# Block products by sevens, summed by chained accumulation in PSUM banks, with an order table per step

## Chip, cores and metric

The kernel runs on one core of one Trainium2 chip. The metric is the device time of one execution in microseconds; the median of the runs is what counts.

## What is computed

The reference is attention over 4 batches of 12 heads, 448 positions and 64 dimensions, followed by two dense layers on the 1792 x 768 result:

```python
x = attention(rmsnorm(q, g_q), rmsnorm(k, g_k), v)   # to [1792, 768]
h = x @ moe_w_in                                     # [768, 2048]
x = (h * sigmoid(h)) @ moe_w_out                     # [2048, 768]
h = x @ moe2_w_in
return (relu(h) ** 2) @ moe2_w_out
```

Inputs are float32. Each matmul operand is split into an upper part (a rounded copy) and a lower part (the rest), and every product is made of three matmuls: upper by upper, lower by upper, upper by lower.

## The kernel before

After attention (up to 223.8 us of the profile) comes layer one in eight segments ("seg": two halves of the 1792 rows, four quarters of the 2048 hidden columns), and then layer two ("end": two halves of the rows, each with eight groups of 2 x 128 hidden columns). A half is two batches of 448 rows, so a moving operand has 448 columns.

**Units.** The product of two blocks of hidden columns with two blocks of the 768 inputs and two batches of rows is an 8-product block product that is made with seven (`seven`, L1197). Its operands are sums of the weights' quarters (`four`, L1153) and of the rows' blocks (`combine`, L1343). Each of the seven products (`prod`, L1199 to L1218) is nine matmuls of 128 x 448, L1209. Product p1 (B11) is copied out of its bank to a tile (`p1_copy`, L604), the other products' banks are added to that tile or to further ones by VectorE (`u_sum`, L1224), and `finish` applies the activation and splits the result. B21 is accumulated in p1's bank behind B11. There are 14 such units in layer one and 16 in layer two.

**Down products.** In layer one (`down`, L1307) a product with the output weights is 12 matmuls of 448 columns, added to a running sum by VectorE (L1320). In layer two a group adds to `total`, 7 chunks of 128 rows by 768 columns. Done plainly (`plain`, L1543) it takes 14 blocks of six matmuls of 384 columns, L1550, each followed by an addition to `total` (`acc`, L1569). In the second half, groups 0 to 6 (`SEVEN2`) take seven products for eight here too (class `products7`, L1573): six of the seven chunks form three pairs, and for each pair products 1 to 7 of three matmuls each, L1674, are made from sums of the hidden blocks (`h_sum`, L1606) and of the output weights (`weights`, L1626). Each product's bank is added to `total` or to four further running sums; the remaining chunk is done plainly. `join` (L1712) adds these running sums up after the last of the seven groups.

**Weights.** The split output weights of layer two (tile w, 768 KB) are stored to a DRAM buffer su in the first half and loaded from it in the second (L1067, L1054); the second half's groups by sevens also load the unsplit words once more.

**Banks.** PSUM's eight banks are split in three rings after attention: "s" (four) for down products, "t" (three) for the seven products, "pv" (one) for p1.

**Halved matmuls.** `columns` (L1106) splits the second matmul of a product in two of 224 columns: in `seven` in products B11 and T4, in `up` always, in `down` in every third output block.

**Order.** Nothing is written in its final order by hand. Every step (a group of instructions with reads and writes) is recorded, and `Plan.forward` (L251) places steps on the engines' queues, taking at each turn the step that can start earliest and, between equals, the one due first. The due times come from a backward pass and tables of offsets by kind of step (`DUE`, `SHIFT`). The queue of an engine is in order: a step that waits holds up those behind it. Attention's steps have fixed nominal times.

Of the kernel before, what the change touches and what calls it, by code (L numbers as in the profile page):

```python
# [9 lines left out]
F32 = mybir.dt.float32  # L10
# [100 lines left out]
class Step:  # L111
# [13 lines left out]
ROUNDS = 8  # L125
AHEAD = 25.0
DUE = {
    "end0": {"acc": 4.25, "down2": -1, "h_hi": 21.25, "h_lo": 3.75, "keep_parts2": -1.25, "load_y": -0.75, "p1_copy": 3.75, "prod": 0.25, "square": 1, "u_sum": -0.5, "w_hi2": -6, "w_lo2": -0.75, "w_sum": -0.75, "y_hi": 5.25, "y_lo": 4.25, "y_sum": -3.5},
    "end1": {"acc": 2, "down2": -11.25, "h_hi": 16, "h_lo": 2.5, "h_sum": -39.5, "join": 18, "keep_parts2": -11.75, "load_parts2": -2.25, "load_word2": 1.75, "load_y": 0.5, "p1_copy": 0.5, "prod": 2, "square": 21.25, "store": -1.25, "u_sum": -1, "w_hi2": 4.25, "w_sum": -4.5, "y_lo": -3, "y_sum": 2.5},
    "now": {"ident": 5.75, "swap_pools": -0.5},  # L130
    "seg0": {"add": -0.5, "down": 3, "g_hi": 0.5, "g_lo": 0.75, "keep": 10.25, "load_raw": -6, "load_y": 0.5, "low": 1, "magnitude": -2, "merge": -6, "out1": -1, "p1_copy": 4, "part": 0.5, "prod": 4.75, "silu": 0.5, "store_y": -1, "u_sum": 2.75, "up": 2.5, "w_hi": 4.5, "w_lo": 6.25, "w_sum": -2, "y_hi": 0.75, "y_lo": 1, "y_sum": 2},
    "seg1": {"add": -4.25, "down": -4.5, "g_hi": 2.25, "g_lo": 5, "keep2": 45.25, "load_raw2": 6, "load_word": -5.5, "load_y": -0.75, "low2": -1.5, "magnitude2": -3, "merge2": -4.5, "p1_copy": -6.25, "part": -3.75, "prod": -3.25, "silu": -5.75, "store_y": 7, "u_sum": 2.25, "w_hi": 1.75, "w_lo": 1, "w_sum": -3, "y_hi": 10, "y_lo": 0.75, "y_sum": 2.5},
}

SHIFT = {
    "seg0": {"down": -3.25, "g_hi": 49, "g_lo": 4.75, "keep": -8.25, "load_raw": -17.5, "load_y": 21.5, "low": -35.5, "merge": 2.5, "part": 20.75, "silu": -0.5, "up": 2.5, "w_lo": 1.25, "y_lo": 3.75, "y_sum": 5.25},
    "seg1": {"add": -11.75, "down": -6, "g_hi": 148, "g_lo": -10.5, "keep": -27.75, "load_raw": -10.5, "low": -7.5, "magnitude": -17.25, "p1_copy": -4.25, "prod": 78.25, "u_sum": 123, "w_hi": 285.25, "w_lo": 29.75, "w_sum": -30.75},
    "seg2": {"add": 1.5, "down": -99.75, "g_hi": 30, "g_lo": 8, "keep": 22.25, "load_raw": -18.75, "low": -73.75, "magnitude": -0.25, "merge": -0.25, "p1_copy": -42, "prod": 14.5, "silu": 17, "u_sum": 27.75, "w_hi": -10, "w_lo": -55, "w_sum": -52.75},
    "seg3": {"down": -205.5, "g_hi": -6.5, "g_lo": 90.25, "keep": 33.25, "load_raw": 1.75, "low": -2.25, "magnitude": -1.25, "merge": -26.5, "out1": -8.5, "p1_copy": -9.5, "prod": 86, "silu": -1.75, "store_y": 4.5, "u_sum": -384.5, "w_hi": -37.75, "w_lo": 31.75, "w_sum": 1.75},
    "seg4": {"down": 9.25, "g_hi": -0.75, "g_lo": -3.25, "keep2": -23.75, "load_raw2": -7.25, "load_word": -15, "load_y": 8, "low2": 2.25, "magnitude2": 1, "merge2": 10.5, "p1_copy": 28.25, "part": 13.5, "prod": 2, "silu": -2, "w_hi": -2.75, "w_lo": 10.75, "w_sum": -13.5, "y_hi": 15.5, "y_lo": -406.5, "y_sum": 155},  # L140
    "seg5": {"add": -41, "down": 69.5, "g_hi": 72.25, "g_lo": 2.5, "keep2": -16, "load_raw2": -136.75, "load_word": -5.5, "low2": 77.25, "magnitude2": -29.5, "merge2": 163.25, "p1_copy": 3.5, "prod": 29, "silu": 10, "u_sum": -10.5, "w_hi": 17.75, "w_lo": 10.25, "w_sum": -101.75},
    "seg6": {"add": 11.75, "down": -291.75, "g_hi": 23.5, "keep2": -10.5, "load_raw2": 0.75, "load_word": -0.75, "low2": 7.75, "magnitude2": 66.75, "merge2": -52.75, "p1_copy": -37.25, "prod": 132, "silu": 193.5, "u_sum": -30.25, "w_hi": 23.25, "w_lo": -29.75, "w_sum": 9.5},
    "seg7": {"down": -5.75, "g_lo": 43.5, "keep2": -43, "load_raw2": 11.5, "load_word": -1.5, "low2": 17.25, "magnitude2": -5, "merge2": 49, "p1_copy": -1.75, "prod": -31, "silu": -27.25, "store_y": -18.25, "u_sum": -169, "w_hi": 57.5, "w_lo": -67.75, "w_sum": -132.25},
    "end-2": {"load_y": -17.25, "y_hi": 328.25, "y_lo": -2, "y_sum": 24.75},
    "end0": {"acc": 0.5, "down2": 3, "h_lo": -10.25, "load_word2": 4.25, "load_y": 4.5, "p1_copy": 4.25, "prod": 57, "relu": 13, "square": 6.75, "u_sum": 0.75, "w_hi2": -3.25, "w_lo2": 3.5, "w_sum": 14.75, "y_hi": 19.75, "y_lo": 21.5, "y_sum": -3.75},
    "end1": {"down2": -28, "h_hi": -1.25, "h_lo": -43.75, "keep_parts2": -19, "load_word2": 34.5, "p1_copy": 10.25, "prod": 0.25, "relu": 34, "square": -41.5, "u_sum": -6.25, "w_hi2": 79, "w_lo2": 89.5, "w_sum": -16},
    "end2": {"acc": -23.75, "down2": 6.5, "h_hi": 55.25, "h_lo": 1.25, "keep_parts2": 8.75, "load_word2": 3, "p1_copy": 21, "prod": 63, "relu": -16.25, "square": 0.5, "u_sum": -2.25, "w_hi2": 17.75, "w_lo2": -57, "w_sum": -15.25},
    "end3": {"acc": 4.25, "down2": 5, "h_hi": -80.5, "h_lo": 0.5, "keep_parts2": 59, "load_word2": 5.25, "p1_copy": 4.25, "prod": 3.5, "relu": -88.75, "square": 16.75, "u_sum": -28.5, "w_hi2": -9.5, "w_lo2": 22.75, "w_sum": -0.25},
    "end4": {"acc": 5.5, "down2": -14.25, "h_hi": 24.25, "h_lo": -11.25, "keep_parts2": 18.25, "load_word2": 10.25, "p1_copy": -69.25, "prod": -4.5, "relu": 5.5, "square": -7.5, "u_sum": 6, "w_hi2": -41.5, "w_lo2": -39.25, "w_sum": 39.25},
# [1641 lines left out]
```

## Time and profile before

| | us |
|---|---|
| median of 3 runs | 1115.44 (1114.39 to 1116.83) |
| profiled execution | 1114.12 |
| its span | 1112.3 |
| attention, up to the first matmul of layer one | 223.8 |
| last matmul starts | 1108.4 |

The span is the time from the first to the last instruction of the profiled execution; the execution's own time is 1.8 us more. The sum of a prediction is made against the profiled execution, which lies 1.3 us below the median. An engine's busy time counts its recorded instructions; matmuls are pipelined, so consecutive ones overlap in the record and their starts give the pitch.

### The profile page before, as it was taken

The numbers are of one execution on the slowest core, as the hardware profiler recorded it, in microseconds if no ns is written. First come the engines' busy times: TensorE is split into PE (matmuls) and PEld (weight loads), VectorE is DVE, ScalarE is ACT, GpSimd is POOL, SyncE is SP. The second block draws the span as 40 slices with busy tenths as digits, with TensorE's granted clock in tenths as the row PEclk, the third lists the DMA queues.
The fourth block names the chain that finished last, engine by engine and source line by source line (L and its number), as shares of the span: only waits on it lengthen the run. The fifth ranks groups of instructions, "written<-read, shape, count | busy, mean of one in ns | idle before, by whom it ended". The sixth has DMA issues, their size and how long they took to land.

```text
span 1112.3 us, 20308 instructions
## 1 busy us (share of the span) xinstructions
PE 1094.0 (98%) x7463; PEld 991.0 (89%) x7463; DVE 910.7 (82%) x1629; ACT 615.9 (55%) x1308; POOL 287.0 (26%) x361
## 2 busy tenths in 40 slices
PE   8999999999999999999999999999999999999998
PEld 6877777699999998999999989999999899999997
DVE  7999999857969689877767896787888877888886
ACT  7999999955645466455445544544333444333221
POOL 5789997300000012000102210022020311222220
PEclk9999999999999999999999999999999999999999
DMA  7344543377655568678776598877878874555453
GB/s 190 102 127 143 150 128 106 116 247 262 195 167 190 177 198 262 199 240 281 252 241 223 177 304 306 302 281 254 317 249 301 276 277 185 185 185 187 169 188 125
DMA packets 122435, 235.29 MB, mean 212 GB/s; under 512 B 12216, under 2 KB 86112, under 8 KB 122336
## 3 DMA queue, kind: packets, MB, share of 16 engines
q1 hardware_dynamic: 122096, 233.80, 63.2%
q8 instruction: 59, 0.97, 0.4%
q14 instruction: 40, 0.33, 0.1%
q10 hardware_dynamic: 240, 0.20, 0.1%
HBM read 157.58 MB, written 76.37 MB: 210 GB/s over the span
## 4 chain that ended last, share of the span: by engine, by line
PE 87%; DVE 7%; issue 2%; ACT 1%; DMA 1%; SPq 0%; POOL 0%; DVEq 0%; ACTq 0%
PE bank L1209 29%; PE bank L1307 20%; PE bank L1550 13%; PE bank L901 7%; PE bank L1674 6%; PE bank L791 4%; PE bank L834 3%; PE bank L1120 3%; PE bank L725 2%; DVE g L1224 1%; PE bank L798 1%; DVE w L625 1%; DVE gg L625 1%; DVE W L1030 1%; DMA w<-sz 0%
## 5 line engine op out<-in xcount | busy, mean ns | idle before, releaser
L1307 PE MATMUL bank<-gg,w 128*128 128x448 f32 (+1 forms) x1168 | 238.3, 363 | 2.4 <-DVE gg L625 1.4
L1307 PEld LDWEIGHTS bank<-gg,w 128*128 128x128 f32 x1168 | 216.3, 188 | 21.5 <-DVE gg L625 2.1
L1224 DVE TENSOR_TENSOR g<-bank,g 128x448 f32<-128x448 f32 x180 | 109.2, 620 | 53.0 <-PE bank L1209 47.9
L1550 PE MATMUL bank<-w,gh 128*128 128x384 f32 (+1 forms) x564 | 142.8, 334 | 0.9 <-DVE gh L618 0.9
L1569 DVE TENSOR_TENSOR gg<-bank,gg 128x384 f32<-128x384 f32 (+1 forms) x197 | 103.7, 551 | 25.0 <-PE bank L1550 24.5
L1209 PE MATMUL bank<-yb,w 128*128 128x448 f32 (+1 forms) x548 | 118.1, 363 | 0.5 <-ACT g L1277 0.5
L616 ACT CAST w<-W 128x768 fp32r<-128x768 f32 (+1 forms) x86 | 64.4, 752 | 96.2 <-PE bank L1550 28.1
L1209 PE MATMUL bank<-xb,w 128*128 128x448 f32 x528 | 115.2, 364 | 0.0
L625 DVE TENSOR_TENSOR w<-W,w 128x768 fp32r<-128x768 f32 (+1 forms) x121 | 105.8, 880 | 6.0 <-ACT w L616 4.9
L1209 PEld LDWEIGHTS bank<-yb,w 128*128 128x128 f32 x548 | 101.3, 188 | 8.6 <-ACT g L1277 0.8
L1209 PEld LDWEIGHTS bank<-xb,w 128*128 128x128 f32 x528 | 98.1, 188 | 7.9
L1550 PEld LDWEIGHTS bank<-w,gh 128*128 128x128 f32 x564 | 101.9, 188 | 2.1 <-DVE gh L618 1.3
L813 DVE TENSOR_REDUCE mx<-bank 128x1 f32<-128x448 f32 x168 | 96.4, 606 | 0.0
L1475 ACT ACTIVATE g<-g 128x448 f32<-128x448 f32 x48 | 27.7, 578 | 123.9 <-DVE g L1224 123.7
L1550 PE MATMUL bank<-w,gl 128*128 128x384 f32 (+1 forms) x282 | 94.2, 334 | 0.0
L821 ACT ACTIVATE E<-bank,mx 128x448 f32<-128x448 f32 x144 | 93.3, 705 | 0.7 <-DVE mx L813 0.2
L625 POOL TENSOR_TENSOR gl<-g,gh 128x448 fp32r<-128x448 f32 (+1 forms) x16 | 14.6, 914 | 188.3 <-ACT gh L616 110.1
L1023 ACT ACTIVATE raw<-raw 128x768 int32<-128x768 uint16 (+1 forms) x72 | 59.5, 826 | 3.0 <-DMA raw<-in_moe_w_in_dram 2.1
L1209 PE MATMUL bank<-xc,w 128*128 128x448 f32 x270 | 59.9, 366 | 0.0
L791 PE MATMUL bank<-T 64*128 64x448 f32 x432 | 54.8, 382 | 2.3 <-ACT T L734 2.1
L625 POOL TENSOR_TENSOR gg<-g,gg 128x448 fp32r<-128x448 f32 x6 | 7.9, 1315 | 183.7 <-ACT gg L616 176.3
L1209 PEld LDWEIGHTS bank<-xc,w 128*128 128x128 f32 x270 | 50.7, 188 | 4.3
(184 smaller groups left out, 2250.7 us busy)
## 6 DMA issues: line engine op xcount, KB each, us to landing
raw<-in_moe_w_in_dram SPq DMA_DIRECT2D x32, 768.0 KB, 5.1
raw<-in_moe_w_out_dram SPq DMA_DIRECT2D x24, 512.0 KB, 4.0
raw<-in_moe_w_out_dram SPq DMA_DIRECT2D x16, 768.0 KB, 6.0
su<-w SPq DMA_DIRECT2D x16, 768.0 KB, 6.3
w<-su SPq DMA_DIRECT2D x16, 768.0 KB
xf<-y SPq DMA_DIRECT2D x48, 224.0 KB, 5.0
xf<-x SPq DMA_DIRECT2D x39, 224.0 KB, 4.9
ki<-W SPq DMA_DIRECT2D x16, 384.0 KB, 6.1
```

Source lines behind the costliest of these rows:

```text
L616: nc.scalar.copy(o(), a())
L625: kind, when, any_t(n, rate), lambda e: engine(e).tensor_tensor(o(), a(), h(), ALU.subtract),
L791: nc.tensor.matmul(pts[j].ap[:, :S], T.ap[r, 0, a, c * CQ:(c + 1) * CQ], T.ap[r, 1, b_], start=(k_ == 0), stop=(k_ == 2),)
L813: lambda e, pt=pt, mx=mx: nc.vector.tensor_reduce(mx.ap, pt.ap[:, :S], AX.X, ALU.max, negate=True),
L821: lambda e, j=j, n=n, pt=pt, mx=mx, E=E: nc.scalar.activation(E.ap[:, j], pt.ap[:, :S], AF.Exp, bias=mx.ap, accum_out=sums.ap[:, n:n + 1]),
L901: nc.tensor.matmul(pv.ap[j * D:(j + 1) * D, q0:q0 + nq], vr.ap[:, j * NCH + m, :], pt.ap[:, j * NCH + m], start=(m == 0), stop=(m == NCH - ...
L1209: nc.tensor.matmul(pt.ap[:, c1:c2], w_()[:, c0 + c, :], view(b, a, c)()[:, c1:c2], start=(start and c == 0 and k == 0), stop=(c == HC - 1 ...
L1224: lambda e: nc.vector.tensor_tensor(o.ap, pt.ap[:, :S], a.ap, ALU.add),
L1307: nc.tensor.matmul(pt.ap[:, c1:c2], w_()[:, f, :], gg.ap[:, k, a, f, c1:c2], start=(f == 0 and n == 0), stop=(f == HQ - 1 and n == 2), ski ...
L1550: nc.tensor.matmul(pt.ap[:, :en], g.ap[:, fi, c0:c0 + P], w_()[:, 0, e0:e0 + en], start=(n == 0), stop=(n == 5),)
L1569: "acc", at, dve_t(n), lambda e: nc.vector.tensor_tensor(o(), pt.ap[:, :n], o(), ALU.add),
L1674: nc.tensor.matmul(pt.ap[:, :NH], a[i][0](m), b[j][0](), start=(start and k == 0), stop=(k == 2), skip_group_check=True,)
```

## The change

1. The groups 1, 3 and 5 of layer two's first half take seven products as well; in the second half the same seven groups do as before.
2. In `seven` the products B11, T2, T3 and T4 are accumulated one behind the other in p1's bank, and the running sum is copied out between them (`take`); T1 and B22 share the bank p5, B21 has p2. Three copies and three additions take the place of one copy and six additions.
3. In `products7.down` the products of a pair share two banks: 1, 6, 7, 4 follow each other in one, 5 and 3 in another (2 has a bank of its own before). Behind each product the bank is added to one block of `total`. The further running sums and `join` go.
4. The split output weights are no longer stored in DRAM; in both halves they are split from the words, which are loaded once per group and serve the sums too.
5. `columns` counts matmuls: it halves the second matmul of a product when more than 150 whole ones have passed, or when matmuls of 384 columns came between.
6. Rings of banks: "s" four and "t" four in layer one; "bu" three, "bv" two and "bx" three in layer two.
7. The due time of every step behind attention is read from a table `LATEST`, one number per step, kind by kind; the backward pass and the offsets go.

```diff
-SEVEN2 = (1,)
+SEVEN2 = {0: (1, 3, 5), 1: range(7)}
+LIST = [(1, 0), (1, 1), (1, 2), (2, 0), (2, 1), (6, 0), (6, 1), (2, 2), (6, 2), (5, 0), (7, 0), (5, 1), (7, 1), (3, 0), (7, 2), (3, 1), (5, 2), (4, 0), (4, 1), (3, 2), (4, 2)]
+KEEP = 150
-BANKS = {"any": (0, 8), "s": (0, 4), "t": (4, 3), "pv": (7, 1)}
+BANKS = {"any": (0, 8), "s": (0, 4), "t": (4, 4), "bu": (0, 3), "bv": (3, 2), "bx": (5, 3)}
...
+LATEST = {
+    "acc": [937, 1072, -3118, 1243, -2011, 894, -2156, 2509,
...
     def schedule(self):
...
+            due.append(-0.25 * LATEST[s.kind][turn[s.kind]])
...
+    since = [KEEP]
+    def columns(second):
+        since[0] += 1
+        if second and since[0] > KEEP:
+            since[0] = 0
+            return [(0, S // 2), (S // 2, S)]
+        return [(0, S)]
...
+        def take():
+            o = sb([P, S], F32, "g")
+            copy_step("p1_copy", at, ("act", "dve"), lambda: o.ap, lambda: p1.ap[:, :S], S, [p1], [o])
+            return o
+        p1, p2, p5 = (psum("t" if at[0] == "seg" else "bx") for _ in range(3))
         product(p1, w0, 0, "B11")
...
+        u1 = take()
+        product(p2, w0, HC, "B21")
+        product(p1, z, HC, "T2", False)
+        u2 = take()
+        product(p5, z, 0, "T1")
+        product(p1, v_, 0, "T3", False)
+        u3 = take()
+        plus(u3, p5)
+        product(p1, a22, 0, "T4", False)
+        c21 = sb([P, S], F32, "g")
+        product(p5, v_, HC, "B22", False)
+        finish(1, 1, u3)
+        finish(1, 0, c21, p1)
+        plus(u1, p2)
+        finish(0, 0, u1)
+        plus(u2, p5)
         finish(0, 1, u2)
...
-                wo = [parts(lambda f=f: second_out(f, at), DM, DM, at, f"u{f}") for f in (f0, f1)]
+                W2 = [second_out(f, at, "V", "yp") for f in (f0, f1)]
+                wo = [parts(lambda W=W: W, DM, DM, at) for W in W2]
...
+            C = {1: (0, 0), 2: (0, 0), 6: (0, 1), 5: (1, 1), 7: (1, 1), 3: (0, 1), 4: (1, 0)}
+            rows = [psum("bu") for m in range(self.npair)]
+            other = {}
+            for n, m in LIST:
+                if n in (2, 5):
+                    other[m] = psum("bv")
+                p = other[m] if n in (2, 5, 3) else rows[m]
+                product(n, m, p, n in (1, 2, 5), t)
+                t += DOWN2 / 4
+                to(*C[n], m, p, n)
```

(`plain` and the products of `products7` set the count of `columns` to 150, so the next product's second matmul is halved.)

The written order shows how the steps move. First the products of a unit on TensorE, in layer two's first half. Before (bank and tile names with their numbers; yb, xb, xc and part hold sums of the rows, w and v those of the weights):

```order
L1209 MATMUL bank5_10711<-yb_8968,w_10624 128x448 x9
L1209 MATMUL bank6_10724<-xb_8964,w_10641 128x448 x9
L1209 MATMUL bank4_10737<-xb_8983,v_10610 128x448
L1209 MATMUL bank4_10737<-xb_8983,v_10610 128x224 x2
L1209 MATMUL bank4_10737<-xb_8983,v_10610 128x448 x7
L1209 MATMUL bank7_10627<-xb_9111,w_10509 128x448 x9
L1209 MATMUL bank5_10774<-xc_9208,w_10624 128x448 x9
L1209 MATMUL bank6_10794<-part_9327,w_10641 128x448 x9
```

In the changed kernel, one of the four places with T3 and T4 next to each other:

```order
L1157 MATMUL bank5_9286<-yb_8917,w_9110 128x448 x9
L1157 MATMUL bank6_9310<-xb_9097,w_9110 128x448
L1157 MATMUL bank6_9310<-xb_9097,w_9110 128x224 x2
L1157 MATMUL bank6_9310<-xb_9097,w_9110 128x448 x7
L1157 MATMUL bank5_9286<-yb_8965,w_9220 128x448 x9
L1157 MATMUL bank7_9346<-xc_9218,w_9220 128x448 x9
L1157 MATMUL bank5_9286<-xb_8884,w_9282 128x448 x9
L1157 MATMUL bank5_9286<-xb_9002,v_9106 128x448 x9
L1157 MATMUL bank7_9346<-part_9308,w_9282 128x448 x9
```

Before, every product but B21 goes to a bank of its own. Now the products to bank5_9286 (B11, T2, T3, T4) stand with one product between them, and the last two with none; on ScalarE the sum behind T3 is copied between them:

```order
L546 COPY g_9323<-bank5_9286 128x448
...
L546 COPY g_9372<-bank5_9286 128x448
L1417 ACTIVATE g_9372<-g_9372 128x448
L1423 ACTIVATE g_9372<-g_9372 128x448
L1417 ACTIVATE g_9403<-bank5_9286 128x448
```

What moved: T4 waits for that copy, which waits for T3's last matmul.

Second, the down products by sevens on TensorE. Before, in the second half of layer two:

```order
L1674 MATMUL bank3_12217<-xb_11339,part_11678 128x384 x3
L1674 MATMUL bank0_12223<-xb_11339,part_11678 128x384 x3
L1674 MATMUL bank1_12229<-xb_11339,part_11678 128x384 x3
L1674 MATMUL bank2_12234<-xb_11339,part_11678 128x384 x3
L1674 MATMUL bank3_12241<-xb_11339,part_11678 128x384 x3
L1674 MATMUL bank0_12246<-xb_11339,part_11678 128x384 x3
```

In the changed kernel, in group 1 of the first half, where a group done plainly stood before (raw holds sums of the weights, part and R those of the hidden blocks):

```order
L1621 MATMUL bank3_9781<-raw_9717,part_9699 128x384 x3
L1621 MATMUL bank4_9787<-raw_9717,part_9699 128x384 x3
L1621 MATMUL bank1_9662<-raw_9777,part_9699 128x384 x3
L1621 MATMUL bank3_9781<-w_9600,part_9699 128x384 x2
L1621 MATMUL bank3_9781<-w_9600,R_9755 128x384
L1621 MATMUL bank4_9787<-w_9600,part_9699 128x384 x2
L1621 MATMUL bank4_9787<-w_9600,R_9755 128x384
L1621 MATMUL bank1_9662<-raw_9717,part_9699 128x384 x3
```

What moved: before, the four banks go round and a bank is written again behind three other products. Now bank3_9781, bank4_9787 and bank1_9662 are each written again behind two, with VectorE's addition of the bank to `total` between.

## Rows read from the trace of the kernel before

**Rows 1.** The page: the span, and the engines' busy time (share of the span).

```profile
span 1112.3 us, 20308 instructions
...
PE 1094.0 (98%) x7463; PEld 991.0 (89%) x7463; DVE 910.7 (82%) x1629; ACT 615.9 (55%) x1308; POOL 287.0 (26%) x361
```

**Rows 2.** Stretches: length, busy us of PE, PEld, DVE, ACT, POOL; PEclk; DMA share; GB/s.

```profile
223.80:685.70 461.90, 459.09 (x2308) 424.04 (x2307) 364.54 (x610) 239.66 (x391) 45.34 (x31) 1.00 0.70 230
685.70:882.00 196.30, 194.34 (x1055) 187.15 (x1054) 158.93 (x276) 85.43 (x146) 30.48 (x18) 1.00 0.78 277
882.00:1108.50 226.50, 223.90 (x1200) 211.93 (x1198) 181.52 (x346) 77.28 (x148) 45.34 (x42) 1.00 0.56 196
```

**Rows 3.** TensorE's timeline in layer one: start, us, what; three products between these.

```profile
363.21 1.99 PE L1209 MATMUL bank<-xb,w 128*128 128x448 f32 x9
...
368.68 7.58 PE L1307 MATMUL bank<-gg,w 128*128 128x448 f32 x36
```

**Rows 4.** TensorE's timeline in layer two; x10 is a product with a halved matmul.

```profile
900.35 2.02 PE L1209 MATMUL bank<-xb,w 128*128 128x448 f32 x9
902.21 2.00 PE L1209 MATMUL bank<-xb,v 128*128 128x448 f32 x10
904.05 1.99 PE L1209 MATMUL bank<-part,w 128*128 128x448 f32 x9
905.88 0.34 PE L1674 MATMUL bank<-xb,gh 128*128 128x384 f32 x1
...
906.94 0.33 PE L1674 MATMUL bank<-xb,gh 128*128 128x384 f32 x1
```

**Rows 5.** TensorE's timeline around a product between plain down products.

```profile
749.32 0.51 PE L1550 MATMUL bank<-w,gh 128*128 128x384 f32 x2
...
749.84 2.02 PE L1209 MATMUL bank<-yb,w 128*128 128x448 f32 x9
751.69 0.51 PE L1550 MATMUL bank<-w,gh 128*128 128x384 f32 x2
...
752.22 0.51 PE L1550 MATMUL bank<-w,gh 128*128 128x384 f32 x2
```

**Rows 6.** Groups by line (count, busy us, mean ns, idle before), whole span, then 685.7 to 882.

```profile
L1224 DVE TENSOR_TENSOR g<-bank,g 128x448 f32<-128x448 f32 x180 | 109.2, 620 | 53.0 <-PE bank L1209 47.9
...
L1569 DVE TENSOR_TENSOR gg<-bank,gg 128x384 f32<-128x384 f32 x84 | 44.6, 552 | 13.5 <-PE bank L1550 13.3
L625 DVE TENSOR_TENSOR w<-W,w 128x768 fp32r<-128x768 f32 x32 | 30.6, 970 | 0.1
```

**Rows 7.** Timelines of TensorE, VectorE and ScalarE, one after the other, 938 to 943 us.

```profile
938.48 2.00 PE L1209 MATMUL bank<-raw,w 128*128 128x448 f32 x10
940.32 0.51 PE L1674 MATMUL bank<-w,gh 128*128 128x384 f32 x2
...
941.73 0.34 PE L1674 MATMUL bank<-w,gl 128*128 128x384 f32 x1
942.42 0.59 PE L1674 MATMUL bank<-w,gh 128*128 128x384 f32 x2 [0.35 <-issue]
...
940.30 1.54 DVE L625 TENSOR_TENSOR xb<-V,xb 128x768 fp32r<-128x768 f32 x1
941.77 1.47 DVE L1569 TENSOR_TENSOR xf<-bank,xf 128x384 f32<-128x384 f32 x3
...
940.57 0.53 ACT L604 COPY g<-bank 128x448 f32<-128x448 f32 x1 [0.64 <-PE bank L1209]
```

**Rows 8.** TensorE's waits: us in total, times, longest.

```profile
PE bank L1674 <- issue: 0.3, 1, 0.3
```

**Rows 9.** DMA issues by tile, then TensorE's timeline at the turn of layer two's halves.

```profile
su<-w SPq DMA_DIRECT2D x16, 768.0 KB, 6.3
w<-su SPq DMA_DIRECT2D x16, 768.0 KB
...
878.25 2.09 PE L1209 MATMUL bank<-raw,w 128*128 128x448 f32 x10 [1.96 <-DMA w<-sw]
```

More of the change, by code (lines that the diff above doesn't have):

```diff
@@ L236, in link @@
                         pre[s.n][t.n] = True
-        late = {b.turn % BANKS["any"][1]: b for b in self.rings["any"]}
-        for tag, (first, n) in BANKS.items():
-            for b in self.rings[tag][:n] if tag != "any" else ():
-                for t in late[first + b.turn].steps:
-                    pre[b.first.n][t.n] = True
+        late = {}
+        for tags in STAGES:
+            last = dict(late)
+            for tag in tags:
+                first, n = BANKS[tag]
+                for b in self.rings[tag]:
+                    k = first + b.turn % n
+                    if b.turn < n and k in last:
+                        for t in last[k].steps:
+                            pre[b.first.n][t.n] = True
+                    late[k] = b
         for s in self.steps:
@@ L420, in stage @@
-        def stage(s):
-            when = s.when[0]
-            return when + str(int(s.when[1] >= {"seg": NQ, "end": self.turn}[when])) if when in ("seg", "end") else when
-        moved = [DUE.get(stage(s), {}).get(s.kind, 0.0) for s in steps]
-        due = [d + x for d, x in zip(due, moved)]
-        best = None
-        got = [None]
-        for _ in range(ROUNDS):
-            end = got[0]
-            got = self.forward(due, end)
-            if best is None or got[0] < best[0]:
-                best, args = got, (due, end)
-            late = self.backward(got[1], got[2])
-            due = [x - y for x, y in zip(moved, late)]
-            self.log = getattr(self, "log", []) + [round(got[0], 1)]
@@ L436, in part @@
-        def part(s):
-            when = s.when[0]
-            if s.nom is not None or when not in ("seg", "end"):
-                return None
-            return when + str(int(s.when[1] if when == "seg" else s.when[1] * 8 / self.turn))
-        due, end = args
-        return self.forward([d + SHIFT.get(part(s), {}).get(s.kind, 0.0) for s, d in zip(steps, due)], end)
+        turn = dict.fromkeys(LATEST, 0)
+        due = []
+        for s in self.steps:
+            if s.nom is not None:
+                due.append(0.0)
+                continue
+            due.append(-0.25 * LATEST[s.kind][turn[s.kind]])
+            turn[s.kind] += 1
@@ L445, in issue @@
+        assert all(len(LATEST[k]) == n for k, n in turn.items())
+        return self.forward(due, END)
     def issue(self):
@@ L1103, in ahead @@
         units.append(at)
-    def columns(halved):
-        return [(0, S // 2), (S // 2, S)] if halved else [(0, S)]
+    since = [KEEP]
[5 more added lines that the diff above has]
+        return [(0, S)]
     def up(x, w, gh, gl, keys, at, cuts):
@@ L1207, in products @@
                     for k, (w_, a) in enumerate(((wh, 0), (wl, 0), (wh, 1))):
-                        for c1, c2 in columns(c == 0 and k == 1 and n in ("B11", "T4")):
+                        for c1, c2 in columns(c == 0 and k == 1):
                             nc.tensor.matmul(
@@ L1305, in products @@
                             for n, (w_, a) in enumerate(((wh, 0), (wl, 0), (wh, 1))):
-                                for c1, c2 in columns(f == 0 and n == 1 and k == 0 and e_ % 3 == 0):
+                                for c1, c2 in columns(f == 0 and n == 1):
                                     nc.tensor.matmul(
@@ L1545, in products @@
         def products(e):
+            since[0] = KEEP
             n = 0
@@ L1573, with __init__ @@
     class products7:
-        def __init__(self, total, left, npair):
+        def __init__(self, total, left, npair, half):
             self.total, self.left, self.npair = total, left, npair
             self.part = sb([P, 2 * NC6 * S // 2], FR, "part", None, "yp")
-            self.block = sb([P, 2 * HC * S], FR, "xb")
-            self.word = [sb([P, UW], FR, "W") for _ in range(2)]
-            self.more = {(n, m): sb([P, S], F32, "xf") for m in range(npair) for n in ("U2", "P7")}
             L = left
@@ L1585, in at @@
                 return lambda: b.ap[:, c0:c0 + n]
+            last = sb([P, S], FR, "R", 2)
             self.S = {
```

255 lines of the change are left out of this document (75 added, 180 removed), and 6 rows, old and new, of the table LATEST.

## Prediction

> **What bounds the kernel now.** I read the first part of the page, then the stretches, then TensorE's timeline, and only then the other engines. The page shows TensorE busy for 98% of the span [rows 1]. The stretches show the same outside attention: TensorE stands idle for 2.8 us of 461.9 in layer one, 2.0 of 196.3 in layer two's first half and 2.6 of 226.5 in the second, with the clock granted in full, while VectorE has 19 to 21% of its time free and ScalarE 48 to 66% [rows 2]. So a matmul left out is time won, work on the other engines costs nothing unless a matmul waits for it, and the little that can be lost is lost in waits. The idle time, 7.4 us, understates these: a matmul is recorded with 0.36 us but the next starts 0.20 later, so about 0.16 of each pause is covered; with some twenty pauses, and 0.1 more before the pitch is back, I put all waits behind attention at about 12 us (an estimate).
>
> The timeline also shows two pitches for the same matmul of 448 columns. In layer one 27 of them take 5.47 us, 0.2026 each [rows 3]. In layer two nine take 1.86, 0.2067 each, until a product with a halved matmul: that one takes 1.84, and the next 1.83 [rows 4]. A stretch that enters from 384-column matmuls is slow, one behind a halved pair is fast.
>
> **The change, part by part.**
>
> *Matmuls left out.* A group of layer two done plainly takes 14 blocks of 6 matmuls, 84 of 384 columns; by sevens 21 products of 3 and 2 blocks of 6, 75. Three groups change: 27 matmuls fewer. Three take 0.52 us, 0.173 each [rows 5]: **−4.7 us**, in places where TensorE is the bound.
>
> *Halved matmuls.* Before, halving follows the name of a product; now the first product behind 384-column matmuls is halved at its second matmul, and otherwise one in some 150. In the written order 458 whole matmuls of 448 columns stand on the slow side before and 51 after: 407 × 0.0041 = −1.7. A halved pair costs 1.84 − 9 × 0.2026 = 0.017 [rows 4]; there are 66 for 84: −0.3. Leaving a fast stretch costs 0.02 (1.06 us for six of 384 columns [rows 4] for the usual 1.04), a slow one 0.01 [rows 5]; before, 27 and 13, now 52 and 0: +0.4. Together **−1.6 us**.
>
> The Trainium skill gives one pitch only ("TensorE: Matmul & The Clock Gate", Back-to-back issue gap): columns over 2.4 GHz plus 2.5 ns, so 189 ns for 448 columns and 162.5 for 384. By that, estimated from that page, the first term would be 4.4 us and this one nothing, together −4.4. The rows differ from it in both, and they decide.
>
> *Sums in banks.* Of the seven products of a unit four now go one after the other into one bank, and ScalarE or VectorE copies the sum out between them: three copies and three additions (30 units) for one copy and six additions. On VectorE layer two loses 46 additions of 0.62 [rows 6], 28.5 us, and ten joins of some 0.6. It gains 33 accumulations of 0.55, 18.2 us [rows 6], and 24 splits of 768 columns of 0.97 [rows 6], 23.3, since output weights are split anew in both halves instead of stored and loaded. Sum: about +7 on the 340 us that VectorE works in layer two [rows 2], so near 83% there, with more of it in the second half. ScalarE gains 26 copies of 0.53 [rows 7], 14 us, and has half its time free. All this I cost at nothing, because matmuls cover it; without that cover it is the third rival below.
>
> *The order of a bank's writes.* Four times in the new order (two in layer one, two in layer two's first half) product T4 stands right behind T3 in the same bank with the copy of that bank between. No such place exists before, so I price it from the nearest rows: the last matmul of a product starts 0.2 before the next row, at 940.12, its copy at 940.57, 0.45 later, and takes 0.53; a matmul that waited started 0.10 behind the read's end (941.77 + 0.55, 942.42) [rows 7]. So 1.08 for a usual 0.20, and 0.08 more for the next pair (0.59 for 0.51 [rows 7]): 0.96 each, **+3.8 us** if all else stays. Lower bound: nothing, where TensorE would have stood idle there for operands anyway, as it does in both layers now.
>
> *Transfers.* Sixteen stores and sixteen loads of 768 KB of split output weights go [rows 9], two loads of 384 KB come: 24 MB of 235 less, and the SP queue is shorter by 30 issues. The one visible wait of TensorE for a load is 1.96 us for w<-sw at the turn of the halves [rows 9]. It may go (−2.1 with its slow restart) or come back elsewhere, since that turn's order is new; bounds −2.1 and +2.1, taken at 0.
>
> *The other waits.* The order of every step behind attention is new, so each of today's waits is redrawn. Price from below: if only the four places and the last group's wait stay, about 8 less. From above: all 12 stay and the four come on top, with some late reads. I take the middle: the new order also holds about 12 us of waits, the four among them. The four are there because nothing else could be started, which is what the present waits are too.
>
> Sum: −4.7 − 1.6 = −6.3. The profiled execution took 1114.12 us and becomes 1107.8; it lies 1.3 below the median shown, so the median becomes **1109.1 us**. Attention, up to 223.8 us, has the same instructions in the same order on every engine.
>
> **Rivals.**
>
> *More goes than the matmuls.* The waits fall to about 4 us, because fewer transfers and fewer additions leave operands ready: 1109.1 − 8 = 1101. For it: half of VectorE's additions to units are gone. Against: it is no less busy in all.
>
> *The saving is eaten.* The four places come on top of all present waits (+3.8) and one or two reads more are late: 1109.1 + 5 = 1114, no difference that can be measured. About 0.2% (2.2 us) is what a measurement of this kernel can tell from no change.
>
> *Slower: the chain in a bank waits for VectorE.* A bank is written again behind at most 1.05 us of other matmuls in 18 places before and 59 after (the four with none among them). A read needs about 1.05 from the last matmul's start to the next; there are 1.2. So one 768-column subtraction (here 1.54 us [rows 7]) ahead in VectorE's queue is a wait: at 941.73 the third matmul is followed only at 942.42, 0.52 late, 0.6 with the restart. It decides from 8 late reads on top of the four (8 × 0.6 + 3.8 − 6.3 = +2.3). With half of the 55 late: 27 × 0.6 + 3.8 − 6.3, some 1129 us. For it: VectorE is fuller in the second half. Against: of the 18 places before one waited visibly [rows 8]. The Trainium skill speaks against chains ("Perfetto Trace Analysis", Matmuls): independent groups should rotate through banks, so that emptying one overlaps the next group's matmuls. By that rule the time is this rival's; the trace agrees where the read was late and disagrees in the other places.
>
> *The halving doesn't do what it says.* If a halved pair behind 384-column matmuls doesn't bring the fast pitch, all of layer two's 1008 stay slow: (1008 − 458) × 0.0041 = +2.3, and the time is about 1112.7. Against: a pair does it inside a run of products [rows 4].
>
> **How the numbers follow.** Forecast, waits within 4 us of today's (1105 to 1113): 0.45. More goes: 0.20. Halving without effect: 0.06. These three are faster by over 0.2% (under 1113.2): 0.71. Eaten: 0.17, the same. VectorE late: 0.12, slower (over 1117.7). The range takes the forecast, nearly all of the first rival and the eaten case with its late reads: 1100.5 (1109.1 − 8.6, waits at 3.5) to 1118 (1109.1 + 3.8 + 5). Outside lie most of the slower case and the end of the first rival, about 0.17.
>
> **What the profile would show.** 27 matmuls of 384 columns fewer and 132 halves for 168. In layer two's products of 448 columns a pitch near 0.2026 behind the first product, and no stretch of 27 at 0.2067. Four pauses near 0.9 us behind a product T3, with a copy of its bank as releaser. No su transfers. Wrong would be: pauses of 0.5 us repeated in each group's down products with VectorE's accumulation as releaser (the slower rival), idle time of TensorE behind attention far from 7.4 us (the waits), or slow stretches that stay (the halving).

## The result and the profile after

The changed kernel took 1123.06 us (median of 4 runs, 1121.03 to 1125.47) and the kernel before 1114.91 on the same chip: ratio 1.0072, 95% interval 1.0059 to 1.0086. It is 8.1 us slower; 1109.1 was forecast, 6.3 below the 1115.4 shown then. The profiled execution took 1123.52, 9.4 more than that of before: 7.4 of it lie in the two layers' matmuls, 1.3 in attention (to 225.1 us for 223.8, with the same instructions), the rest at the end.

The page of the changed kernel:

```profile
span 1121.4 us, 20181 instructions
...
PE 1094.7 (98%) x7418; PEld 986.1 (88%) x7418; DVE 936.2 (83%) x1648; ACT 639.6 (57%) x1354; POOL 292.6 (26%) x370
```

TensorE has 45 instructions fewer than in [rows 1] and is busy for longer; VectorE's busy time rose by 25.5 us. The stretches, columns as in [rows 2]: layer one, layer two's first half, second half:

```profile
225.10:694.10 469.00, 464.13 (x2285) 425.29 (x2284) 374.29 (x622) 246.75 (x397) 45.61 (x31) 1.00 0.74 244
694.10:890.50 196.40, 189.27 (x1014) 178.39 (x1013) 164.93 (x280) 89.10 (x164) 41.53 (x36) 1.00 0.49 173
890.50:1117.20 226.70, 223.10 (x1217) 212.59 (x1215) 190.46 (x349) 90.09 (x170) 39.81 (x33) 1.00 0.41 141
```

TensorE now stands idle for 4.9, 7.1 and 3.6 us, 15.6 against 7.4 in [rows 2]. The granted clock is 1.00 in all three stretches, so the time was lost in waits.

To compare runs I use three numbers worked out from all records of a trace. *Stream*: from the first to the last matmul start of the two layers; the attention ahead of it has the same instructions in every run and ended between 222.2 and 225.1 us. *Waits*: what lies between two successive matmul starts beyond the usual pitch (0.2026 for 448 columns, 0.173 for 384), summed where it is over about 15 ns more than the slow pitch (0.2067); the restart behind a pause counts. *Stretched*: VectorE instructions behind attention that took over 0.1 us longer than the lower quartile of their line, operation and size, and by how much in all.

| run | time, us | stream | waits | stream less waits | stretched |
|---|---|---|---|---|---|
| before | 1114.91 | 884.64 | 12.8 | 871.8 | 29, 14.8 us |
| the change | 1123.06 | 892.07 | 25.3 | 866.8 | 46, 31.7 us |
| e1 change, GpSimd sets | 1109.09 | 878.03 | 12.3 | 865.7 | 7, 2.5 us |
| e2 before, GpSimd sets | 1110.90 | 882.29 | 10.4 | 871.9 | 5, 2.2 us |
| e3 change, copies elsewhere | 1115.41 | 886.57 | 20.0 | 866.5 | 48, 31.8 us |
| e4 before, halving by count | 1113.44 | 885.04 | 14.6 | 870.4 | 31, 16.2 us |
| e5 change, GpSimd held back | 1109.67 | 880.35 | 13.9 | 866.5 | 40, 17.5 us |
| e6 before, GpSimd held back | 1111.34 | 882.83 | 11.0 | 871.8 | 25, 9.9 us |
| e7 change, e1 and e3 | 1102.67 | 873.44 | 7.2 | 866.2 | 8, 3.3 us |
| e8 change, e5 and more halving | 1109.83 | 879.86 | 13.1 | 866.7 | 38, 17.1 us |
| e9 change, held back behind any | 1123.94 | 893.15 | 27.4 | 865.8 | 58, 36.3 us |

The matmuls themselves became 5.0 us shorter, nearly as forecast, and the waits 12.5 us longer.

One thing more stands in the stream and the waits of seven of these traces (e1 to e6 and e9): the granted clock fell to 0.50 behind the wait at the turn of layer two's halves, and the matmuls there took 1.5 to 1.6 us more in all. The traces of the kernel before, the change, e7 and e8 don't have it. Stretches of e1 and of the change behind that wait, columns as in [rows 2]:

```profile
875.00:878.00 3.00, 3.00 (x10) 2.68 (x9) 0.62 (x1) 1.00 (x2) 0.00 (x0) 0.53 1.00 403
...
886.60:889.00 2.40, 2.21 (x11) 2.09 (x12) 2.03 (x4) 0.86 (x3) 0.00 (x0) 1.00 1.01 412
889.00:892.00 3.00, 3.00 (x17) 2.78 (x16) 1.25 (x2) 1.49 (x4) 0.00 (x0) 1.00 0.99 394
```

Whether an edit brings the fall or chance does isn't shown: the kernel before and e7 have waits like those of e2 and e1 without it. Where a trace with the fall is compared with one without, 1.5 us are taken off below ("at equal clock"). The times in the table are medians of several executions, of which one is traced.

TensorE's waits in the profile of after:

```profile
PE bank L1157 <- ACT g L546: 4.3, 7, 0.7
PE bank L1157 <- DVE w L567: 2.5, 3, 1.0
PE bank L1157 <- ACT g L1417: 2.0, 1, 2.0
...
PE bank L1157 <- DVE g L548: 1.5, 2, 1.0
...
PE bank L1621 <- DVE gg L1510: 1.1, 3, 0.5
PE bank L1621 <- DVE w L567: 1.1, 1, 1.1
```

L546 (ScalarE) and L548 (VectorE) are the copies between chained products; L567 is the split's subtraction on VectorE, L1510 the addition to `total`, which the chains of the down products wait for. (The 2.0 us behind L1417 stand at the turn of the halves, where [rows 9] have a load of w as releaser.) Two kinds stand out: copies of chained banks, and operands that VectorE delivers late. For the first, one of the four places with T3 and T4 next to each other, TensorE's timeline and then ScalarE's:

```profile
682.44 1.78 PE L1157 MATMUL bank<-xb,w 128*128 128x448 f32 x8
684.84 1.49 PE L1157 MATMUL bank<-xb,v 128*128 128x448 f32 x6 [0.62 <-ACT g L546]
...
684.26 0.53 ACT L546 COPY g<-bank 128x448 f32<-128x448 f32 x1 [3.08 <-PE bank L1157]
```

For the second, one place in the second half, timelines of VectorE, GpSimd and TensorE:

```profile
1043.98 2.81 DVE L567 TENSOR_TENSOR gl<-g,gh 128x448 fp32r<-128x448 f32 x2
1046.71 0.95 DVE L567 TENSOR_TENSOR w<-V,w 128x768 fp32r<-128x768 f32 x1
...
1044.05 2.25 POOL L567 TENSOR_TENSOR w<-V,w 128x768 fp32r<-128x768 f32 x1 [16.38 <-ACT w L558]
...
1046.30 0.34 PE L1621 MATMUL bank<-w,gh 128*128 128x384 f32 x1
1047.71 0.45 PE L1621 MATMUL bank<-w,gh 128*128 128x384 f32 x1 [1.08 <-DVE w L567]
```

Two subtractions of 448 columns take 2.81 us; such a pair takes 1.15 elsewhere. The second, by its own record from 1044.51, began while a GpSimd subtraction ran and took 2.28, 1.66 too long. The next split of w is late by that, and TensorE waits 1.24 us from its usual start. All 53 of these subtractions, and 63 splits of w, behind attention (count, busy us, mean ns):

```profile
L567 DVE TENSOR_TENSOR w<-W,w 128x768 fp32r<-128x768 f32 x63 | 62.6, 995 | 3.6 <-ACT w L558 2.7
...
L567 DVE TENSOR_TENSOR gl<-g,gh 128x448 fp32r<-128x448 f32 x53 | 38.0, 743 | 1.6 <-ACT gh L558 1.5
```

### The profile page after: what moved, and what is told of

Same layout as the page of the kernel before. It is cut to its first block, busy times and chain, and to the rows that moved or that the text cites. A ratio compares the mean times of both kernels' runs of the same rounds, so it can differ in the third digit from the quotient of the medians.

```text
span 1121.4 us, 20181 instructions
## 1 busy us (share of the span) xinstructions
PE 1094.7 (98%) x7418; PEld 986.1 (88%) x7418; DVE 936.2 (83%) x1648; ACT 639.6 (57%) x1354; POOL 292.6 (26%) x370
## 2 busy tenths in 40 slices
DMA packets 118114, 210.89 MB, mean 188 GB/s; under 512 B 11736, under 2 KB 85632, under 8 KB 118016
## 4 chain that ended last, share of the span: by engine, by line
PE 81%; DVE 13%; ACT 2%; issue 2%; DMA 1%; SPq 0%; POOL 0%; DVEq 0%; ACTq 0%
PE bank L1157 24%; PE bank L1248 20%; PE bank L1491 9%; PE bank L1621 8%; PE bank L843 7%; PE bank L733 4%; PE bank L776 3%; PE bank L1068 3%; DVE gl L567 2%; DVE w L567 2%; PE bank L667 2%; DVE gg L1510 1%; PE bank L740 1%; DVE g L1172 1%; DVE w L560 1%
## 5 line engine op out<-in xcount | busy, mean ns | idle before, releaser
L1248 PEld LDWEIGHTS bank<-gg,w 128*128 128x128 f32 x1161 | 216.3, 188 | 18.9 <-DVE part L1261 0.8
L1510 DVE TENSOR_TENSOR gg<-bank,gg 128x384 f32<-128x384 f32 x287 | 148.7, 550 | 40.6 <-PE bank L1491 27.4
L1157 PE MATMUL bank<-xb,w 128*128 128x448 f32 (+1 forms) x533 | 114.7, 362 | 0.2 <-DVE g L1172 0.2
L1491 PE MATMUL bank<-w,gh 128*128 128x384 f32 (+1 forms) x420 | 106.2, 334 | 0.7 <-ACT gh L558 0.7
L546 ACT COPY g<-bank 128x448 f32<-128x448 f32 x75 | 39.8, 530 | 111.3 <-PE bank L1157 110.4
L567 DVE TENSOR_TENSOR w<-W,w 128x768 fp32r<-128x768 f32 (+1 forms) x108 | 93.5, 868 | 4.2 <-ACT w L558 2.9
L558 ACT CAST w<-W 128x768 fp32r<-128x768 f32 (+1 forms) x62 | 46.5, 751 | 66.0 <-DVE W L972 14.2
L1491 PEld LDWEIGHTS bank<-w,gh 128*128 128x128 f32 x420 | 75.8, 188 | 1.5 <-ACT gh L558 1.1
L1172 DVE TENSOR_TENSOR g<-bank,g 128x448 f32<-128x448 f32 x90 | 55.5, 617 | 23.4 <-ACT g L546 14.8
L567 POOL TENSOR_TENSOR w<-W,w 128x768 fp32r<-128x768 f32 (+1 forms) x10 | 17.2, 1725 | 207.0 <-DVE w L560 194.1
L1491 PE MATMUL bank<-w,gl 128*128 128x384 f32 (+1 forms) x210 | 70.3, 335 | 0.2 <-DVE gl L567 0.2
L965 ACT ACTIVATE raw<-raw 128x768 int32<-128x768 uint16 (+1 forms) x72 | 59.8, 830 | 14.2 <-DMA raw<-in_moe_w_in_dram 10.7
L1157 PE MATMUL bank<-xc,w 128*128 128x448 f32 (+1 forms) x278 | 60.1, 361 | 0.8 <-DVE w L567 0.8
L1417 ACT ACTIVATE g<-g 128x448 f32<-128x448 f32 x48 | 27.8, 579 | 46.7 <-DVE g L1172 46.5
```

What stands on the lines that cost most here:

```text
L567: kind, when, any_t(n, rate), lambda e: engine(e).tensor_tensor(o(), a(), h(), ALU.subtract),
L965: lambda e: nc.scalar.activation(lo(), raw.ap[:, :2 * m].bitcast(U16).rearrange("p (m t) -> p m t", t=4)[:, :, 1], AF.Copy, bias=2.0 ** -1 ...
L1157: nc.tensor.matmul(pt.ap[:, c1:c2], w_()[:, c0 + c, :], view(b, a, c)()[:, c1:c2], start=(start and c == 0 and k == 0), stop=(c == HC - 1 ...
L1172: lambda e: nc.vector.tensor_tensor(o.ap, pt.ap[:, :S], o.ap, ALU.add),
L1248: nc.tensor.matmul(pt.ap[:, c1:c2], w_()[:, f, :], gg.ap[:, k, a, f, c1:c2], start=(f == 0 and n == 0), stop=(f == HQ - 1 and n == 2), ski ...
L1491: nc.tensor.matmul(pt.ap[:, :en], g.ap[:, fi, c0:c0 + P], w_()[:, 0, e0:e0 + en], start=(n == 0), stop=(n == 5),)
```

## The experiments

**Theory 1**: GpSimd's instructions hold VectorE's, and the held ones make operands and bank reads late. **Theory 2**: the chains in banks are the cost, whatever VectorE does. In the runs this means the chains of the units (`seven`); those of the down products were taken away in none.

### e1, e2: GpSimd's subtractions and sums become memsets

```diff
+    def two_of(e, o, a, b, op):
+        if e == "pool" and plan.now > 222.0:
+            nc.gpsimd.memset(o.bitcast(F32), 0.0)
+            return
+        engine(e).tensor_tensor(o, a, b, op)
...
-            ... lambda e: engine(e).tensor_tensor(o(), a(), h(), ALU.subtract),
+            ... lambda e: two_of(e, o(), a(), h(), ALU.subtract),
```

(so in every such step of the two layers, in e1 on the changed kernel, in e2 on the one before; what GpSimd would have computed is zeros then.)

> The changed kernel, all orders as they are; behind attention each subtraction or sum that GpSimd makes is replaced by a memset of the same columns on GpSimd (so lower parts and sums made there are zeros). Theory 1 (GpSimd): in the changed kernel 46 VectorE instructions behind attention took 31.7 us longer than their like while a GpSimd instruction ran (before the change 29, 14.8 us), most by 0.82 us each, and they make operands and bank reads late. Then most of these stretches go, TensorE's waits behind attention fall from 25.3 us to about 13 and the time from 1123 to about 1111. Theory 2 (chains): the waits are the price of writing one bank product after product; waits stay above 22 us, time within 2 us of 1121.

> The same edit in the kernel before, as a control. Theory 1: 14.8 us of stretches go; waits fall from 12.8 us by 3 to 6, time from 1115 to about 1110. So the edit is worth some 12 us behind the change and some 5 before it. Theory 2: waits fall by 1 to 2 us in either kernel.

e1 took 1109.09 us, 0.9951 of the kernel before (0.9937 to 0.9964), e2 1110.90, 0.9962 (0.9950 to 0.9974). So the edit is worth 14.0 us in the changed kernel and 3.5 to 4 in the one before. The same two groups in e1 (the subtraction is on L472 here), and then the same place:

```profile
L472 DVE TENSOR_TENSOR w<-W,w 128x768 fp32r<-128x768 f32 x63 | 60.0, 954 | 4.2 <-ACT w L565 3.4
...
L472 DVE TENSOR_TENSOR gl<-g,gh 128x448 fp32r<-128x448 f32 x53 | 31.4, 618 | 2.4 <-ACT gh L565 2.2
```

```profile
1030.03 1.15 DVE L472 TENSOR_TENSOR gl<-g,gh 128x448 fp32r<-128x448 f32 x2
1031.10 0.95 DVE L472 TENSOR_TENSOR w<-V,w 128x768 fp32r<-128x768 f32 x1
...
1032.35 0.51 PE L1628 MATMUL bank<-w,gh 128*128 128x384 f32 x2
```

The mean falls from 743 to 618 ns, the pair takes 1.15, and TensorE doesn't wait. Theory 1 holds in size: waits 25.3 to 12.3 (13 was expected; 10.8 at equal clock), time 1109 (1111). In e2 the waits fell by 2.4, at equal clock by 3.9 (3 to 6 was expected), and the time was as expected. Without GpSimd's holds the change is 1.8 us faster than the kernel before, which the intervals of the two ratios don't tell from nothing; by the stream it is 4.3.

A memset of 384 columns takes 0.42 us where the subtraction takes 1.02, so e1 also delivers GpSimd's results sooner. No wait of TensorE in the two layers of the change is put down to GpSimd by the profile, and e5 below leaves GpSimd's work as it is.

### e3: the copies between the products read elsewhere

```diff
-            copy_step("p1_copy", at, ("act", "dve"), lambda: o.ap, lambda: p1.ap[:, :S], S, [p1], [o])
+            copy_step("p1_copy", at, ("act", "dve"), lambda: o.ap, lambda: view(x["T4"], 0, 0)().bitcast(F32), S, [p1], [o])
```

> The changed kernel, all orders as they are; the three copies between the chained products of a unit read a block of the same size in SBUF (an operand of the unit's later product T4) and not the bank, so that no product waits for a copy and no copy for a product (the sums are then wrong ones). Theory 2: the waits with such a copy as their releaser, about 9 us with their restarts (the four places T3 to T4 among them, 3.6), all go: waits 16 us, time about 1113. Theory 1: the four places go (3.6), of the others most of the time is lost a little later for the operands that are late anyway: waits 20 to 21 us, time about 1118.

It took 1115.41 us, 1.0011 (1.0001 to 1.0020): 7.7 less than the change, 5.5 by the stream. The place shown above has no pause any more; T4 starts 1.63 us behind the first of eight matmuls:

```profile
675.73 1.79 PE L1157 MATMUL bank<-xb,w 128*128 128x448 f32 x8
677.36 1.99 PE L1157 MATMUL bank<-xb,v 128*128 128x448 f32 x9
```

Waits are 20.0, what theory 1 expected, but 18.5 at equal clock, and so between the two, as the time is. The stretches are nearly those of the change (48, 31.8 us). So the units' chains have a price of their own, 7.0 us by the stream at equal clock, though not the main one. Of the down products' chains, which stay in e3, the waits of the change name an addition to `total` three times, with 1.1 us (L1510 above).

### e4: the new rule for halving in the kernel before

```diff
-                        for c1, c2 in columns(c == 0 and k == 1 and n in ("B11", "T4")):
+                        for c1, c2 in columns(c == 0 and k == 1):
```

(with the counting `columns` of the change, and the count set by `plain` and `products7`.)

> The kernel before with the new rule for halved matmuls alone; order and waits as they are. By the prediction's term of 1.6 us: layer two's 444 matmuls of 448 columns at 0.2067 fall below 80, time 1113.4. By what the changed kernel's trace shows in layer one (275 matmuls in slow stretches behind waits, none before): layer two gains 1.5, layer one loses up to 1.1 behind its waits, time 1113.5 to 1115.

1113.44 us, 0.9984 (0.9975 to 0.9994). Layer two's 444 slow matmuls are gone, none of its longer runs is slow any more; layer one has one slow stretch of 167. The stream less waits falls by 1.4, and the waits rise by 1.8, of which 1.5 are the clock's fall. So the term of 1.6 us is there in the pitch, and at equal clock 1.1 of it in the stream. The time is too coarse to size it: the medians differ by 0.9 us, the interval goes from 0.7 to 2.8.

### e5, e6: GpSimd's steps held to their place in the sequence

The scheduler counts VectorE's subtractions, sums and SBUF copies and GpSimd's work as excluding each other, and puts GpSimd's beside VectorE's bank reads. On the chip nothing enforces that: each queue starts its next step when its operands are there. In 30 of the 46 stretches (24.3 of 31.7 us) GpSimd's start, trace less plan, was over 0.8 us earlier than VectorE's.

```diff
+            new = nc.cur_bb.bb.instructions[-1]
+            if at[n] == "dve" and s.on["dve"][2]:
+                locked = new
+            if at[n] == "pool" and s.nom is None and start[n] > 222.0:
+                tc.add_manual_dep(new, locked.name, behind, reason="plan")
```

> The changed kernel, computing all of it, all orders as they are; behind attention each GpSimd step also waits for the last VectorE subtraction, sum or SBUF copy that stands before it in the scheduler's own sequence. The scheduler counts such work of the two engines as excluding each other; on the chip GpSimd starts as soon as its operands are there, ahead of its place (in 30 of the 46 stretches GpSimd ran over 0.8 us earlier against the plan than VectorE did). Theory 1a: the stretches are these early starts; of 31.7 us over half go, waits fall from 25 to 15-18 us, time 1113 to 1116. Rival 1b: the scheduler's order has no room for GpSimd's work at all, held back it only delivers its own results late; waits stay above 22, time within 3 us of 1123.

> The same in the kernel before. Theory 1a: of 14.8 us of stretches some go; time 1112 to 1114 (taking all of them away gave 3.5). Rival 1b: 1114 to 1117.

e5 took 1109.67 us, 0.9950 of the kernel before (0.9937 to 0.9962); e6 1111.34, 0.9960 (0.9945 to 0.9976). None of the held steps starts early any more in either (two GpSimd steps of attention, which aren't held, still do, 0.8 and 0.9 us of stretches). At the place shown, timelines of VectorE, GpSimd and TensorE:

```profile
1032.86 1.15 DVE L576 TENSOR_TENSOR gl<-g,gh 128x448 fp32r<-128x448 f32 x2
...
1035.41 0.62 DVE L1181 TENSOR_TENSOR g<-bank,g 128x448 f32<-128x448 f32 x1
1035.95 1.06 DVE L1519 TENSOR_TENSOR gg<-bank,gg 128x384 f32<-128x384 f32 x2
...
1035.63 1.86 POOL L576 TENSOR_TENSOR w<-V,w 128x768 fp32r<-128x768 f32 x1 [18.69 <-DVE gl L576]
...
1035.18 0.51 PE L1630 MATMUL bank<-w,gh 128*128 128x384 f32 x2
```

GpSimd's split now starts behind the two subtractions, beside bank reads that keep their usual 0.62 and 2 x 0.53 us, and takes 1.86 instead of 2.25. Theory 1a holds and 1b doesn't, though the sizes came out otherwise: stretches fall by 14.2 us, 45% and not over half (40 are left, shorter ones), while waits are 13.9 (15 to 18 was expected) and both times are better than expected, e6 by 0.7 us. e5 computes all of it, is 13.4 us under the change, and its interval lies below the kernel before. Against e6, the kernel before with the same dependency, it is 1.7 us less, which the intervals don't tell from nothing (2.5 by the stream).

### e7: both edits together

The diffs of e1 and e3.

> The changed kernel with both earlier edits: GpSimd's subtractions and sums behind attention are memsets, and the three copies between a unit's products read an operand in SBUF and not the bank. It prices the chains with VectorE undisturbed: of the 12.3 us of waits left without GpSimd's holds, 5 name such a copy (four places 3.6, the rest 1.4). If that is all the chains cost: time about 1104 to 1105, stream of matmuls 873. If the four places only stand where operands are late anyway: less than 2 us off 1109.

1102.67 us, 0.9888 (0.9875 to 0.9901), less than expected, with the stream as expected. Against e1 that is 6.4 less, by the stream 4.6, by the waits 5.1; of the latter two 1.5 are the clock's fall, which e1 has and e7 has not, and the 3.6 of waits that are left are as much as the four places cost. With e1 and e3 it makes a square. At equal clock, taking the holds away gives 15.6 us of stream with chains and 11.6 without, taking the chains away 7.0 with holds and 3.0 without: some 4 us go by either edit. The waits say where: copies between chained products (L546 and L548) end nine waits in the change, 5.8 us, but five in e1, where the ScalarE copy is on L553:

```profile
PE bank L1164 <- ACT g L553: 3.0, 5, 0.6
```

By the medians the two add up more nearly (14.0 and 12.7, 7.7 and 6.4). So each has a price of its own; whether they are separate in full, one trace per run doesn't settle.

### e8: more halved matmuls

`KEEP = 36` on top of e5.

> As the first of these four (GpSimd held back), and a product's second matmul halved behind 36 whole ones instead of 150, since slow stretches of 448 columns stand behind waits in layer one (275 matmuls there, 1.1 us) until the next halved pair. Some 50 pairs more at 0.017 (+0.9); gains 0.5 to 1.1: time within 0.5 us of the first.

1109.83 us, 0.9951 (0.9939 to 0.9964): as e5, and as expected. Slow matmuls in layer one fall from 171 to 90 (81 × 0.0041 = 0.3 us); the 37 further halved pairs cost some 0.6 (at 0.017, an estimate).

### e9: GpSimd held behind any VectorE instruction

```diff
-            if at[n] == "dve" and s.on["dve"][2]:
+            if at[n] == "dve":
```

> The changed kernel as with GpSimd held back, but each GpSimd step behind attention waits for the last VectorE instruction of any kind that stands before it in the scheduler's sequence, those that read a bank too. Bank-reading instructions were never stretched (none of 96 that began while GpSimd ran), so if the hold on subtractions, sums and SBUF copies is what counts, nothing more is to be won: stretches stay near 17.5 us, time 1109 to 1111. If GpSimd's place against VectorE as a whole counts: stretches under 12 us, time 1107 to 1108.

1123.94 us, 1.0071 (1.0055 to 1.0086), beside 1.0072 of the change: both expectations missed. Now GpSimd waits for the very bank read that was to run beside it, and runs into the next subtraction. Of VectorE's bank reads 55 began while GpSimd ran (92 in e5), of the other VectorE instructions 67 (47 in e5). The two groups again:

```profile
L576 DVE TENSOR_TENSOR w<-W,w 128x768 fp32r<-128x768 f32 x63 | 65.0, 1033 | 4.9 <-ACT w L567 4.0
...
L576 DVE TENSOR_TENSOR gl<-g,gh 128x448 fp32r<-128x448 f32 x53 | 36.0, 704 | 0.5 <-ACT gh L567 0.5
```

No wait of TensorE in e9's two layers is put down to GpSimd by the profile, so it isn't GpSimd's own results that TensorE waits for. What counts is not that GpSimd is kept back, but beside which VectorE instruction it runs. Over e1, e5, the change and e9, stretches of 2.5, 17.5, 31.7 and 36.3 us go with waits of 12.3, 13.9, 25.3 and 27.4: the same order, but not in proportion, since e5's 17.5 cost little more than e1's 2.5.

## Why the prediction was wrong, point by point

**Matmuls left out (−4.7): right.** The intervals behind matmuls of 384 columns number 1275 before and 1248 after, 27 fewer.

**Halved matmuls (−1.6): right in layer two, not seen in layer one.** Timeline of the changed kernel, layer one behind a wait and then layer two:

```profile
301.63 2.12 PE L1157 MATMUL bank<-yb,w 128*128 128x448 f32 x9 [1.02 <-DVE g L548]
303.58 2.02 PE L1157 MATMUL bank<-xc,w 128*128 128x448 f32 x9
305.44 2.02 PE L1157 MATMUL bank<-yb,w 128*128 128x448 f32 x9
...
708.69 2.00 PE L1157 MATMUL bank<-xb,w 128*128 128x448 f32 x10
710.52 1.99 PE L1157 MATMUL bank<-xc,w 128*128 128x448 f32 x9
712.35 1.99 PE L1157 MATMUL bank<-xb,v 128*128 128x448 f32 x9
```

In layer two the first product, with a halved pair, takes 1.83 and the next 1.83: the fast pitch. Layer two's slow matmuls fall from 444 to 69 (375 × 0.0041 = 1.5). But behind the wait at 301 us the product at 303.58 takes 1.86, the slow pitch, until the next halved pair, 93 matmuls later. Layer one has 275 slow ones where it had none in longer runs (1.1 us), since a wait can begin a slow stretch and the count now lets 150 pass before the next halved pair. In e1, with fewer waits, the stream less waits is 6.2 us below e2's and before's: the whole −6.3.

**The four places (+3.8): right.** Each takes 0.78 to 0.79 longer and 0.10 to 0.11 more at the next matmul: 0.89 four times, 3.6 for 3.8. All the units' chains together cost 7.0 us by the stream at equal clock, and 3.0 where GpSimd doesn't hold VectorE. The Trainium skill's rule to rotate banks ("Perfetto Trace Analysis", Matmuls) was right to that extent: e3 and e7 price the breach of it.

**Sums in banks, VectorE (+7, costed at nothing): the sum nearly right, the price not.** VectorE's busy time in layer two went from 340.5 us [rows 2] to 355.4, by 14.9, of which 9.4 are stretches (9.5 before, 18.9 after); the work itself rose by 5.5. "All this I cost at nothing, because matmuls cover it" left out that VectorE doesn't have its time to itself.

**Transfers (0): right.** The su transfers are gone, 235.29 MB became 210.89, and the wait at the turn stayed (2.1 before, 2.2 after, from its usual start).

**The other waits: here the prediction failed.** It took "the new order also holds about 12 us of waits, the four among them". With GpSimd's holds taken out (e1) or GpSimd kept in its place (e5) that is so: 12.3 and 13.9. As the kernel stands they are 25.3, and the sign that the prediction named for this came: TensorE's idle time is 15.6 us and not near 7.4. I read VectorE, ScalarE and TensorE against each other and GpSimd not at all, though a row of mine showed the hold: the subtraction of 768 columns at 940.30 took 1.54 us [rows 7], where its like takes 0.95. GpSimd's timeline of the kernel before has the instruction that ran when it began:

```profile
940.01 1.02 POOL L625 TENSOR_TENSOR W<-g,part 128x384 fp32r<-128x384 f32 x1
```

I used the 1.54 as the length of a late read and did not ask what had made it long.

**The rival "the chain in a bank waits for VectorE"** had the sign, with 0.12, and a part of the mechanism: on top of the four places the waits of the change name eight late reads of a bank (five copies of units, three additions to `total`), just the number from which it decided, 5.7 us from start to start. What it lacked is the rest, and the cause. Nine waits, 6.4 us, are for a split's subtraction on VectorE (L567) that comes late with no chain in between. And it took a fuller VectorE for the reason: in e1, where VectorE has the same work, one of the eight and two of the nine are left, 1.1 us. Without the units' chains (e3) the stretches are the same and cost 13.1 us of stream (e3 less e7; 11.6 at equal clock).

**What stays open.** GpSimd has 98 scheduled steps behind attention in place of 89, and VectorE's time in instructions that can be held rose by some 41 us at their usual lengths (about 456 to 497), that in bank reads fell from 300 to 268, since additions from banks became accumulation and splits came in. That goes with twice the stretches. But by the stream 14.0 us reached TensorE from 31.7 of stretches after the change (15.6 at equal clock), and 2.4 from 14.8 before (3.9). Whether the new order table or the lesser slack of the new structure makes that share larger was not tried. Nor was the changed kernel run without the chains of the down products.

## What to carry to other kernels

Before a change that shifts work between VectorE instructions that read banks and such that read SBUF twice, look in the trace at what GpSimd does meanwhile: compare one instruction's duration with its like, and look for a GpSimd record over the longer ones. A scheduler's assumption that two engines exclude each other holds on the chip only where a dependency enforces it; one dependency per GpSimd step gave 13 us in the changed kernel and 4 in the one before. A stretch that should be bound by TensorE is worth as much as its waits leave: price the new order's waits by their releasers, engine by engine, before taking the old sum over.

## What the runs showed of the hardware

- **GpSimd holds some VectorE instructions and not others.** Behind attention in the changed kernel, of 47 VectorE instructions with two SBUF operands that began while GpSimd ran (over 0.1 us before its end) 38 were stretched, of 8 SBUF copies all 8, of 96 that read a bank none (none of 122 before). Beside a GpSimd instruction of 384 columns (1.02 us when undisturbed) 18 of 27 stretches were 0.80 to 0.84 us long; the longest were 0.97 beside 448 columns (1.15) and 1.66 beside 768 (1.85): as if VectorE waited until GpSimd is nearly done. In e1, where GpSimd only sets, 1 of 17 with two SBUF operands was stretched. The Trainium skill says that the two share SBUF interfaces, with contention for VectorE instructions in a two-port mode or with two SBUF inputs ("GPSIMD Engine Reference", Key points); the trace agrees for two SBUF inputs and gives the price.
- **The clock fell behind the wait at the turn of the halves.** It occurs in 7 of the 11 profiled executions, of either kernel, behind waits of 2.1 to 2.6 us, and in 4 it doesn't behind like ones (2.1 to 2.4). In e5 (columns as above):

```profile
872.00:874.00 2.00, 1.15 (x6) 0.72 (x4) 2.00 (x3) 1.41 (x3) 0.32 (x1) 1.00 0.82 307
...
876.00:878.00 2.00, 2.00 (x7) 1.73 (x7) 1.14 (x2) 0.00 (x0) 0.00 (x0) 0.50 0.99 407
...
880.00:882.00 2.00, 2.00 (x12) 1.85 (x11) 1.23 (x2) 0.41 (x1) 0.16 (x1) 1.00 1.01 350
```

  TensorE waited for a load from 873 to 875.4; at 876 to 878 the granted clock was 0.50, the lower level (1.2 GHz), and nine intervals of 448 columns were 0.17 us longer, 1.5 us in all.
- **A pause can change the pitch of the matmuls behind it**, in either direction: in the change the wait at 301 us begins a slow stretch (0.2066), the one at 463 us ends one (0.2059, then 0.2027). And a halved pair doesn't always bring the fast one: in e4 the 167 matmuls from 223.3 us, right behind a halved pair, took 0.2067.
